# Transposing attention output by the DMA crossbar in a fused sliding/dilated attention and MLP kernel

## The chip, the cores and the metric

The kernel runs on one core of a Trainium2 chip. The metric is device time in microseconds, the median of repeated executions; less is better. The profile is of one execution on the same core.

## The reference

Attention over 8 batch rows, 8 heads, 576 positions, head dimension 64, followed by an MLP with a squared ReLU over all 4608 tokens. Heads 0 to 3 look back over a window of 32 positions; heads 4 to 7 look back over 128 positions and see every fourth one.

```python
batch, n_heads, seq, head_dim = (8, 8, 576, 64)
rel = pos[:, None] - pos[None, :]
mask_plain = (rel >= 0) & (rel < 32)
mask_dil = (rel >= 0) & (rel < 128) & (rel % 4 == 0)
attn = softmax(where(mask, q @ k.T / 8, -1e9));  o = attn @ v
x = o.transpose(0, 2, 1, 3).reshape(4608, 512)
g = np.maximum(x @ w_in, 0) ** 2        # w_in: 512 x 2048
out = g @ w_out                          # w_out: 2048 x 512
```

Inputs and output are float32; the kernel computes with float16 operands and float32 sums.

## The kernel before

**Two streams of work on TensorE.** The attention of one batch row (index `b`, 0 to 7) is interleaved by hand with the MLP of one chunk of 512 tokens. The MLP of chunk `c` is a Python generator (`moe_gen`) that issues a few matmuls and then yields; `pump(n)` lets it run n steps. From chunk 2 on a chunk has 60 steps: 32 for the first matrix product (`mm1_gen`: two for each of 16 blocks of the hidden dimension) and 28 for the second (`mm2_strassen_gen`, which uses seven half-size products in the PSUM banks `pa`, `pb` and `pc`). Bank `pa` is filled four times: after each filling ScalarE copies it out (`take`, line 387, tiles `ou` and `ov`), and the next filling must wait for that copy. The fillings end with steps 36, 42, 50 and 56.

While row `b` is computed, the pending generator is that of chunk `b - 1`. Tokens are numbered row after row, 576 to a row, so chunk `b - 1` needs rows up to `b - 1` alone, and chunk `b` needs the first `512 - 64 b` tokens of row `b`.

**One row of attention**, in program order:

- `pump(first)`: 24, 16, then 8 steps for rows 2, 3 and 4 on.
- `attn_scores`: `s_sliding` twice, `s_dilated` twice; each makes scores transposed (keys on partitions), then ScalarE's exponential (line 547) and VectorE's product with a mask (line 548). Each is followed by `pump(gap)`, with gap 4 in row 2 and 3 later.
- `attn_values`: three `av_sliding` (each two blocks of 96 queries, four heads) and four `av_dilated` (queries of two of the four residue classes, halves `t` of 72 queries). `normalize` divides by the softmax sum on VectorE (lines 590 and 591) and gives x with tokens on partitions. `x_sliding` (tile `px`) and `x_dilated` (tile `py`) transpose x on TensorE into PSUM, and ScalarE copies it to `xT` (lines 640 and 658). `xT` has features on partitions, as the first MLP product wants it, and keeps four rows of tokens. `pump(gap2)` stands between the parts, with 2 in row 2 and 3 later.
- `pump(1000)`: the rest of the chunk's steps.

**Loads.** For row `b + 1`, during row `b`: GpSimd's queue loads q and k of the sliding heads (`ns`) and rewrites those of the dilated ones in DRAM (`dd`), after `after_transposes` has seen the last QK transpose of the row before land (`seen`, line 231). At hook 3, after the second `s_dilated`, `turn` runs: `by_token` on VectorE reorders `ns` to `nr`; then SyncE's queue issues the write of `nr` to DRAM (`dp`), the loads of v (`sv`, `sd`), the DMA transposes of `dp` into `QKTp` and of `dd` into `QKTd`; GpSimd casts v (`cast_v`). The results of each chunk (`leave`, tiles `ou`, `ov`) are stored by SyncE's queue too.

Rows 0 and 1 are written out separately: they transpose q and k on TensorE and run before or between the first chunks.

PSUM: two tiles of two banks for attention (`pa` by function name, tag "pa"), and four single banks for the MLP and for `px` and `py` (tag "pm").

Of the kernel before, what the change touches and what calls it, by code (L numbers as in the profile page):

```python
# [17 lines left out]
def kernel(  # L18
# [28 lines left out]
    NB = S // QB  # L47
    PADP = P - QB
    CL = S // DIL
    QD = CL // 2  # L50
    PADD = (48, P - QD)
    OWND = (CL - 64, 64)
    KPAD = 64
    UW = 576

# [1 line left out]
    wpool = ctx.enter_context(tc.tile_pool(name="wpool", bufs=1))  # L57
    stg = ctx.enter_context(tc.tile_pool(name="stg", bufs=1))
    natp = ctx.enter_context(tc.tile_pool(name="natp", bufs=2))
    xp = ctx.enter_context(tc.tile_pool(name="xp", bufs=4))  # L60
    gp = ctx.enter_context(tc.tile_pool(name="gp", bufs=2))
    osb = ctx.enter_context(tc.tile_pool(name="osb", bufs=3))
    otp = ctx.enter_context(tc.tile_pool(name="otp", bufs=3))
# [68 lines left out]

    def load_dilated_v(b, eng):
        vv = v[b, HH:H].rearrange("h (i c) d -> i h (c d)", c=DIL)
        i0 = 0
        for t in range(2):
            eng.dma_start(out=sd[P - OWND[t] : P, t, :, :], in_=vv[i0 : i0 + OWND[t]])
            i0 += OWND[t]

    def load_v(b):  # L140
        load_sliding_v(b)
# [114 lines left out]
    md = maskd.rearrange("p (n t w) -> p n t w", t=2, w=QD)  # L256
    for m, w, pad in (
        (maskp.rearrange("p (n w) -> p n w", w=QB), QB, PADP),
        (md[:, :, 0], QD, PADD[0]),
        (md[:, :, 1], QD, PADD[1]),  # L260
    ):
# [305 lines left out]
    def s_dilated(b, g):  # L567
        tiles = [pa(f"pz{b}_{g}_{h}") for h in range(2)]
        for h, ps in enumerate(tiles):
            for a in range(2):  # L570
                for t in range(2):
                    q0 = KPAD + (2 * g + h) * CL + QD * t
                    for e in range(2):
                        r = slice(D * e, D * (e + 1))
                        n = 2 * a + t
                        nc.tensor.matmul(  # L576
                            ps[:, e, QD * n : QD * (n + 1)],
                            QKTd[b % 2][r, 1, a, q0 - PADD[t] : q0 - PADD[t] + P],
                            QKTd[b % 2][r, 0, a, q0 : q0 + QD],
                            start=True,  # L580
                            stop=True,
                        )
        for h, ps in enumerate(tiles):
            softmax(4 + 2 * g + h, ps, maskd)

    def normalize(b, what, pav, w):
        x = xp.tile([QB, 2, HH, D], FP16, name=f"x{b}_{what}", tag="x")
        rcp = xp.tile([QB, 2, HH], FP32, name=f"rcp{b}_{what}", tag="rcp")
        pv = pav[0:w, :, 0 : HH * (D + 2)].rearrange("p i (h d) -> p i h d", d=D + 2)
        nc.vector.reciprocal(rcp[0:w], pv[:, :, :, D])  # L590
        nc.vector.tensor_tensor(  # L591
            out=x[0:w],
            in0=pv[:, :, :, 0:D],
            in1=rcp[0:w].unsqueeze(3).to_broadcast([w, 2, HH, D]),
            op=ALU.mult,
        )
        return x

    def av_sliding(b, mp):
# [12 lines left out]
        return normalize(b, f"p{mp}", pav, QB)  # L612

    def av_dilated(b, t, a):
        pav = pa(f"paw{b}_{t}_{a}")
        for e in range(2):
            for h in range(HH):
                off = e * 288 + a * 144 + t * QD
# [7 lines left out]
        return normalize(b, f"d{t}_{a}", pav, QD)  # L626

    def x_sliding(b, half, xs, wide):
        px = pt(f"px{b}_{half}", wide)
        for m3 in range(3):  # L630
            m = 3 * half + m3
            x = xs[m // 2][:, m % 2].rearrange("p h d -> p (h d)")
            for c in range(2):
                nc.tensor.transpose(  # L634
                    px[:, 288 * c + QB * m3 : 288 * c + QB * (m3 + 1)],
                    x[:, P * c : P * (c + 1)],
                    ident[0:QB, 0:QB],
                )
        t0 = (b * S + 288 * half) % XW
        nc.scalar.copy(  # L640
            xT[:, 0:2, t0 : t0 + 288],
            px[:, 0:UW].rearrange("x (c t) -> x c t", c=2),
        )

    def x_dilated(b, t, xs, wide):
        py = pt(f"py{b}_{t}", wide)
        for a in range(2):
            for e in range(2):
                x = xs[a][:, e].rearrange("p h d -> p (h d)")
                for c in range(2):  # L650
                    o = 288 * c + QD * (2 * a + e)
                    nc.tensor.transpose(  # L652
                        py[:, o : o + QD],
                        x[0:QD, P * c : P * (c + 1)],
                        ident[0:QD, 0:QD],
                    )
        t0 = (b * S + 288 * t) % XW
        nc.scalar.copy(  # L658
            xT[:, 2:4, t0 : t0 + 288].rearrange("x c (i r) -> x c i r", r=DIL),
            py[:, 0:UW].rearrange("x (c r i) -> x c i r", c=2, r=DIL),  # L660
        )

    def attn_scores(b, gap, less=0, hooks={}):
        for hp in range(2):
# [10 lines left out]
            pump(gap - less)  # L675

    def attn_values(b, gap, wide=False, hooks={}):
        xs = []
        for mp in range(3):
            xs.append(av_sliding(b, mp))  # L680
            if mp < 2:
                halo_sliding(b, mp + 1)
            else:
                halo_dilated(b, 0)
            if 4 + mp in hooks:
                hooks[4 + mp]()
            pump(gap)
        x_sliding(b, 0, xs, wide)
        halo_dilated(b, 2)
        pump(gap)  # L690
        ys = [av_dilated(b, 0, 0)]
        pump(gap)
        x_sliding(b, 1, xs, wide)
        pump(gap)
        ys.append(av_dilated(b, 0, 1))
        pump(gap)
        zs = []
        for a in range(2):
            zs.append(av_dilated(b, 1, a))
            pump(gap)  # L700
        x_dilated(b, 0, ys, wide)
        pump(gap)
        x_dilated(b, 1, zs, wide)


    n, m = nsd[0]
# [16 lines left out]
        t_dilated(0, m, a, False)  # L723
    halo_sliding(0, 1)
    pump(1)
    xs = [av_sliding(0, 0)]
    pump(1)
    for g in range(2):
        s_dilated(0, g)
# [14 lines left out]
    dd = keep_dilated_qk(2)  # L744
    nr = by_token(2, ns)
    for mp in (1, 2):
        xs.append(av_sliding(0, mp))
        pump(1)
    x_sliding(0, 0, xs, False)
    pump(1)  # L750
    ys = [av_dilated(0, 0, 0)]
    pump(1)
    x_sliding(0, 1, xs, False)
    pump(1)
    pending.clear()
# [30 lines left out]
    for b in range(2, B):  # L786
# [56 lines left out]
```

The softmax here doesn't subtract the row's maximum and nothing guards it: scores larger than these inputs give would overflow.

## Time and profile before

| | |
|---|---|
| median of 3 runs | 311.45 us (311.31 to 311.76) |
| profiled execution | 309.11 us, its span on the core 307.3 us |
| TensorE busy | 290.7 us (95%) |
| VectorE, ScalarE, GpSimd busy | 207.9, 183.4, 71.7 us |
| px transposes (line 634) | 96, with ScalarE copies of 0.638 us to `xT`, 16 |
| py transposes (line 652) | 128, with ScalarE copies of 0.638 us to `xT`, 16 |
| QKTp, QKTd DMA transposes | 12 each, 288 KB, median to landing 6.5 and 3.9 us |
| TensorE clock granted | full throughout |

The span reaches from the first to the last instruction; the time also has what lies around it. In the profile a group is named by line, engine and operation, then what it writes and reads (`xT<-py`), with buffer numbers left out. SPq is SyncE issuing DMAs; a time to landing runs from the start of the issue until all data has arrived. Consecutive matmuls overlap, so the time that a group costs TensorE is the distance from its start to the start of the next one, not the duration of one.

### The profile page before, as it was taken

To read this page: it belongs to the slowest core of one execution; us is meant where nothing else is said; L and a number is where in the kernel's file an instruction comes from. 1 tells how busy PE (TensorE), PEld (TensorE's weight loads), DVE (VectorE), ACT (ScalarE), POOL (GpSimd) and SP (SyncE) were. 2 spreads that over 40 slices of the span, in tenths; PEclk is the share of its full clock that TensorE was granted. 3 is DMA by queue.
4 is the path that set the end of the run, shared out by engine and by line. 5 is a ranking of instruction groups with operands and counts; after the bars stand their busy time and mean duration, and the time that the engine had idled before them with its cause. 6 is when DMAs were issued, how large, how long until landed. Compare 5 with 4: busy or idle time off the path is not lost.

```text
span 307.3 us, 7108 instructions
## 1 busy us (share of the span) xinstructions
PE 290.7 (95%) x2874; PEld 196.5 (64%) x2874; DVE 207.9 (68%) x433; ACT 183.4 (60%) x326; POOL 71.7 (23%) x114
## 2 busy tenths in 40 slices
PE   1798998999999999999999999999999999999994
PEld 1454554554455469656998997569756975785583
DVE  7784448568953798489748983898378934834652
ACT  2766648668645982598339834983499336425620
POOL 4481008413805303400630083007000000000000
PEclk9999999999999999999999999999999999999999
DMA  7899997999699999999968996889500020003004
GB/s 116 188 200 213 206 171 114 189 241 205 112 214 194 222 199 185 240 154 191 171 130 188 181 184 97 219 166 186 165 10 2 0 109 29 0 4 136 2 0 137
DMA packets 67024, 43.58 MB, mean 142 GB/s; under 512 B 48624, under 2 KB 59376, under 8 KB 66992
## 3 DMA queue, kind: packets, MB, share of 16 engines
q1 hardware_dynamic: 57920, 28.45, 44.9%
q0 software_dynamic: 9072, 14.68, 27.7%
q8 instruction: 22, 0.36, 0.5%
q14 instruction: 10, 0.08, 0.1%
HBM read 36.70 MB, written 16.52 MB: 173 GB/s over the span
## 4 chain that ended last, share of the span: by engine, by line
PE 71%; ACT 10%; DVE 7%; DMA 6%; issue 2%; SPq 2%; POOL 1%; POOLq 0%; DVEq 0%
PE ph L294 27%; PE pa L371 16%; PE pb L371 8%; PE po L437 7%; ACT AT L547 5%; DMA ns<-in_q_dram 5%; PE pc L371 4%; ACT rt L317 3%; PE paw L619 3%; PE pav L605 2%; PE px L634 1%; PE py L652 1%; DVE AT L548 1%; DMA QKTp<-dp 1%; PE pf L491 1%
## 5 line engine op out<-in xcount | busy, mean ns | idle before, releaser
L294 PE MATMUL ph<-xT,wi 128*128 128x512 f16 (+1 forms) x640 | 133.4, 359 | 0.7 <-ACT xT L658 0.7
L317 ACT ACTIVATE rt<-ph 128x512 f16<-128x512 f32 x144 | 84.9, 603 | 33.5 <-PE ph L294 33.5
L294 PEld LDWEIGHTS <-wi 128*128 128x128 f16 x640 | 68.6, 114 | 46.8 <-issue 0.8
L318 DVE TENSOR_TENSOR g<-rt 128x512 f16<-128x512 f16 x144 | 62.2, 435 | 42.7 <-ACT rt L317 41.1
L371 PEld LDWEIGHTS <-g 128*128 128x128 f16 x448 | 42.5, 98 | 5.3
L170 POOL CAST vp<-sv 128x512 f16<-128x512 f32 x24 | 17.5, 760 | 108.6 <-DMA sv<-in_v_dram 62.1
L371 PEld LDWEIGHTS <-gs 128*128 128x128 f16 x336 | 31.6, 98 | 3.7 <-DVE gs L328 0.3
L437 PE MATMUL po<-wo,g 128*128 128x512 f16 x128 | 33.1, 379 | 0.0
L398 DVE TENSOR_TENSOR ov<-pb,ov 128x512 f32<-128x512 f32 x14 | 9.7, 691 | 29.9 <-PE pb L371 18.2
L371 PE MATMUL pa<-wt,gs 128*128 128x256 f16 x224 | 28.5, 273 | 0.0
L371 PE MATMUL pb<-wt,g 128*128 128x256 f16 x224 | 27.7, 273 | 0.0
L178 POOL CAST vd<-sd 128x512 f16<-128x512 f32 (+1 forms) x32 | 24.2, 782 | 3.1 <-DMA sd<-in_v_dram 2.4
L387 ACT COPY ov<-pa 128x512 f32<-128x512 f32 x14 | 8.2, 585 | 26.8 <-PE pa L371 26.8
L591 DVE TENSOR_TENSOR x_d<-paw,rcp_d 72x512 f16<-72x512 f32 x32 | 22.0, 687 | 1.1
L547 ACT ACTIVATE AT<-pz 128x576 f16<-128x576 f32 x32 | 20.0, 712 | 1.7 <-PE pz L576 1.6
L548 DVE TENSOR_TENSOR AT<-AT,maskp 128x576 f16<-128x576 f16 x32 | 17.3, 545 | 5.1 <-ACT AT L547 2.6
L547 ACT ACTIVATE AT<-ps 128x576 f16<-128x576 f32 x32 | 19.2, 662 | 1.2 <-PE ps L557 0.9
L658 ACT COPY xT<-py 128x576 f16<-128x576 f16 x16 | 10.2, 640 | 14.7 <-PE py L652 14.6
L591 DVE TENSOR_TENSOR x_p<-pav,rcp_p 96x512 f16<-96x512 f32 x24 | 16.5, 687 | 0.8
L387 ACT COPY ou<-pa 128x512 f32<-128x512 f32 x14 | 8.2, 588 | 14.5 <-PE pa L371 14.5
L548 DVE TENSOR_TENSOR AT<-AT,maskd 128x576 f16<-128x576 f16 x32 | 14.9, 484 | 2.6 <-ACT AT L547 0.6
L640 ACT COPY xT<-px 128x576 f16<-128x576 f16 x16 | 10.2, 638 | 9.2 <-PE px L634 8.6
(81 smaller groups left out, 306.6 us busy)
## 6 DMA issues: line engine op xcount, KB each, us to landing
sv<-in_v_dram SPq DMA_DIRECT2D x14, 288.0 KB, 6.2
dp<-nr SPq DMA_DIRECT2D x12, 288.0 KB, 4.1
out_dram<-ou SPq DMA_DIRECT2D x6, 512.0 KB, 3.1
out_dram<-ov SPq DMA_DIRECT2D x6, 512.0 KB, 3.5
sd<-in_v_dram SPq DMA_DIRECT2D x8, 320.0 KB, 7.3
ns<-in_k_dram POOLq DMA_DIRECT2D x8, 288.0 KB, 5.2
ns<-in_q_dram POOLq DMA_DIRECT2D x8, 288.0 KB, 6.4
sd<-in_v_dram SPq DMA_DIRECT2D x8, 256.0 KB, 6.7
```

Of the source, the lines that this page charges most:

```text
L170: nc.gpsimd.tensor_copy(vp[b % 2][:, m : m + 2, :, 0:D], sv[:, :, m : m + 2, :].rearrange("p h m d -> p m h d"))
L178: nc.gpsimd.tensor_copy(vd[b % 2][p0:P, t, c : c + 2, :, 0:D], sd[p0:P, t, :, D * c : D * (c + 2)].rearrange("p h (c d) -> p c h d", d=D),)
L294: nc.tensor.matmul(ph[:, t0:t1], wi4[ffc // 4][:, dmk, :, ffc % 4], xT[:, dmk, x0 : x0 + t1 - t0], start=(dmk == 0 and t0 == 0), stop=(dmk ...
L317: nc.scalar.activation(rt, ph[:], ACTF.Relu)
L318: nc.vector.tensor_mul(g[:, ffc, :], rt, rt)
L371: nc.tensor.matmul(banks[bank][:, t], a(k, t), b(k), start=(new and t == 0 and k == 0), stop=(k == HF - 1), skip_group_check=True,)
L387: nc.scalar.copy(ot, banks[A])
L437: nc.tensor.matmul(po, g[:, ffc, t * P : (t + 1) * P], wo[ffc // 4][:, ffc % 4, :], start=(ffc == 0), stop=(ffc == NFF - 1),)
L547: nc.scalar.activation(AT[:, u, 0:UW], ps[:, :, 0 : UW // 2], ACTF.Exp, scale=scale)
L548: nc.vector.tensor_mul(AT[:, u, 0:UW], AT[:, u, 0:UW], mask)
L591: nc.vector.tensor_tensor(out=x[0:w], in0=pv[:, :, :, 0:D], in1=rcp[0:w].unsqueeze(3).to_broadcast([w, 2, HH, D]), op=ALU.mult,)
L640: nc.scalar.copy(xT[:, 0:2, t0 : t0 + 288], px[:, 0:UW].rearrange("x (c t) -> x c t", c=2),)
```

## The change

From row 3 on, `attn_values_by_dma` takes the place of `attn_values`. x stays in SBUF tiles with tokens on partitions, and four DMA transposes a row (SBUF to SBUF, issued by SyncE) take the place of 28 PE transposes. The two of the sliding heads write straight into `xT`. The two of the dilated heads write a tile `yd` in which each residue class is contiguous; ScalarE then interleaves the classes into `xT` (`x_from`). Rows 0 to 2 keep the PE transposes.

The halves of a residue class's 144 queries become 80 and 64, in place of 72 and 72 (`QD`, `Q0D`, `PADD`), in all rows; masks, scores, values and transposes follow. `normalize` writes into tiles that `x_tiles` gives: `xs` (96 x 2 x 6 x 2 x 64) and `xd` (80 or 64 x 4 x 4 x 64), two buffers of each.

`turn` is cut in three. At hook 3 it still reorders, writes `dp` and loads v. `turned` (the QKTp transposes) comes after the sliding x transposes, and `done` (the QKTd transposes and the casts of v) after the dilated ones. In row 2 both follow `attn_scores` at once.

```diff
-    QD = CL // 2
-    PADD = (48, P - QD)
-    OWND = (CL - 64, 64)
+    QD = (80, 64)
+    Q0D = (0, 80)
+    PADD = (48, 64)
...
-    xp = ctx.enter_context(tc.tile_pool(name="xp", bufs=4))
+    xp = ctx.enter_context(tc.tile_pool(name="xp", bufs=2))
+    yp = ctx.enter_context(tc.tile_pool(name="yp", bufs=1))
...
-                    q0 = KPAD + (2 * g + h) * CL + QD * t
+                    q0 = KPAD + (2 * g + h) * CL + Q0D[t]
...
-                            ps[:, e, QD * n : QD * (n + 1)],
+                            ps[:, e, o : o + QD[t]],
...
-    def normalize(b, what, pav, w):
-        x = xp.tile([QB, 2, HH, D], FP16, name=f"x{b}_{what}", tag="x")
...
+    def normalize(b, what, pav, w, x):
...
+        if x.shape[2] < HH:
+            pv, rb = [y.rearrange("p i (c e) d -> p i c e d", c=2) for y in (pv, rb)]
+        nc.vector.tensor_tensor(out=x, in0=pv, in1=rb, op=ALU.mult)
...
+    def x_tiles(b):
+        x = xp.tile([QB, 2, NB, 2, D], FP16, name=f"xs{b}", tag="xs")
+        return x, [xp.tile([QD[t], DIL, HH, D], FP16, name=f"xd{b}_{t}", tag=f"xd{t}") for t in range(2)]
...
+    def x_from(b, t, y):
+        t0 = b * S % XW + DIL * Q0D[t]
+        o = xT[:, 2:4, t0 : t0 + DIL * QD[t]].rearrange("x c (i r) -> x c i r", r=DIL)
+        nc.scalar.copy(o, y.rearrange("x r c i -> x c i r"))
+
+    def x_sliding_by_dma(b, xs):
+        t0 = b * S % XW
+        for c in range(2):
+            nc.sync.dma_start_transpose(
+                out=xT[:, c, t0 : t0 + S].rearrange("x (m q) -> x m q", q=QB),
+                in_=xs[0][:, c].rearrange("p m e d -> p (m e d)"),
+            )
+
+    def x_dilated_by_dma(b, t, xs):
+        y = yp.tile([P, DIL, 2, QD[t]], FP16, name=f"yd{b}_{t}", tag=f"yd{t}")
+        nc.sync.dma_start_transpose(
+            out=y.rearrange("x r c i -> x (r c) i"), in_=xs[1][t].rearrange("p r h d -> p (r h d)")
+        )
+        return y
...
+    def attn_values_by_dma(b, gap, then=(None, None)):
+        xs = x_tiles(b)
+        for mp in range(3):
+            av_sliding(b, mp, xs)
+            if mp < 2:
+                halo_sliding(b, mp + 1)
+            else:
+                for c in (0, 2):
+                    halo_dilated(b, c)
+            pump(gap)
+        x_sliding_by_dma(b, xs)
+        if then[0]:
+            then[0]()
+        ys = []
+        for t in range(2):
+            for a in range(2):
+                av_dilated(b, t, a, xs)
+                pump(gap)
+            ys.append(x_dilated_by_dma(b, t, xs))
+        if then[1]:
+            then[1]()
+        for t in range(2):
+            pump(7 if b > 3 else 5)
+            x_from(b, t, ys[t])
...
             def turn():
-                dp = keep_sliding_qk(nxt, by_token(nxt, ns))
+                kept.append(keep_sliding_qk(nxt, by_token(nxt, ns)))
                 load_v(nxt)
-                transpose_sliding(nxt, dp)
+
+            def turned():
+                transpose_sliding(nxt, kept[0])
+
+            def done():
                 transpose_dilated(nxt, dd)
                 cast_v(nxt)
...
-        attn_values(b, gap2, False, hooks)
+        if b == 2:
+            turned()
+            done()
+            attn_values(b, gap2)
+        else:
+            attn_values_by_dma(b, gap2, (turned, done) if nxt < B else (None, None))
```

More of the change, by code (lines that the diff above doesn't have):

```diff
@@ L134, in load_dilated_v @@
         vv = v[b, HH:H].rearrange("h (i c) d -> i h (c d)", c=DIL)
-        i0 = 0
         for t in range(2):
-            eng.dma_start(out=sd[P - OWND[t] : P, t, :, :], in_=vv[i0 : i0 + OWND[t]])
-            i0 += OWND[t]
+            eng.dma_start(out=sd[P - QD[t] : P, t, :, :], in_=vv[Q0D[t] : Q0D[t] + QD[t]])
     def load_v(b):
@@ L255 @@
     hi_ = const.tile([P, QB], FP16, name="hi_")
-    md = maskd.rearrange("p (n t w) -> p n t w", t=2, w=QD)
+    md = maskd.rearrange("p (n w) -> p n w", w=CL)
     for m, w, pad in (
         (maskp.rearrange("p (n w) -> p n w", w=QB), QB, PADP),
-        (md[:, :, 0], QD, PADD[0]),
-        (md[:, :, 1], QD, PADD[1]),
+        (md[:, :, 0 : QD[0]], QD[0], PADD[0]),
+        (md[:, :, QD[0] : CL], QD[1], PADD[1]),
     ):
@@ L571, in s_dilated @@
                 for t in range(2):
-                    q0 = KPAD + (2 * g + h) * CL + QD * t
+                    q0 = KPAD + (2 * g + h) * CL + Q0D[t]
                     for e in range(2):
                         r = slice(D * e, D * (e + 1))
-                        n = 2 * a + t
+                        o = CL * a + Q0D[t]
                         nc.tensor.matmul(
-                            ps[:, e, QD * n : QD * (n + 1)],
+                            ps[:, e, o : o + QD[t]],
                             QKTd[b % 2][r, 1, a, q0 - PADD[t] : q0 - PADD[t] + P],
-                            QKTd[b % 2][r, 0, a, q0 : q0 + QD],
+                            QKTd[b % 2][r, 0, a, q0 : q0 + QD[t]],
                             start=True,
@@ L584, in s_dilated, with av_sliding @@
             softmax(4 + 2 * g + h, ps, maskd)
-    def normalize(b, what, pav, w):
-        x = xp.tile([QB, 2, HH, D], FP16, name=f"x{b}_{what}", tag="x")
-        rcp = xp.tile([QB, 2, HH], FP32, name=f"rcp{b}_{what}", tag="rcp")
+    def normalize(b, what, pav, w, x):
+        rcp = xp.tile([P, 2, HH], FP32, name=f"rcp{b}_{what}", tag="rcp")
         pv = pav[0:w, :, 0 : HH * (D + 2)].rearrange("p i (h d) -> p i h d", d=D + 2)
         nc.vector.reciprocal(rcp[0:w], pv[:, :, :, D])
[L591 to L599, printed above, removed]
+        pv = pv[:, :, :, 0:D]
+        rb = rcp[0:w].unsqueeze(3).to_broadcast([w, 2, HH, D])
+        if x.shape[2] < HH:
[4 more added lines that the diff above has]
+        return x, [xp.tile([QD[t], DIL, HH, D], FP16, name=f"xd{b}_{t}", tag=f"xd{t}") for t in range(2)]
+    def av_sliding(b, mp, xs):
         pav = pa(f"pav{b}_{mp}")
@@ L611, in av_sliding, with av_dilated @@
                 )
-        return normalize(b, f"p{mp}", pav, QB)
-    def av_dilated(b, t, a):
+        normalize(
+            b, f"p{mp}", pav, QB, xs[0][:, :, 2 * mp : 2 * mp + 2].rearrange("p c m e d -> p m c e d")
+        )
+    def av_dilated(b, t, a, xs):
         pav = pa(f"paw{b}_{t}_{a}")
@@ L617, in av_dilated @@
             for h in range(HH):
-                off = e * 288 + a * 144 + t * QD
+                off = e * 288 + a * CL + Q0D[t]
                 nc.tensor.matmul(
@@ L625, in av_dilated @@
                 )
-        return normalize(b, f"d{t}_{a}", pav, QD)
+        normalize(b, f"d{t}_{a}", pav, QD[t], xs[1][t][:, 2 * a : 2 * a + 2])
     def x_sliding(b, half, xs, wide):
@@ L630, in x_sliding @@
         for m3 in range(3):
-            m = 3 * half + m3
-            x = xs[m // 2][:, m % 2].rearrange("p h d -> p (h d)")
             for c in range(2):
@@ L635, in x_sliding @@
                     px[:, 288 * c + QB * m3 : 288 * c + QB * (m3 + 1)],
-                    x[:, P * c : P * (c + 1)],
+                    xs[0][:, c, 3 * half + m3].rearrange("p e d -> p (e d)"),
                     ident[0:QB, 0:QB],
@@ L646, in x_dilated @@
         py = pt(f"py{b}_{t}", wide)
[L647 to L660, printed above, removed]
+        w = QD[t]
+        for r in range(DIL):
+            x = xs[1][t][:, r].rearrange("p h d -> p (h d)")
+            for c in range(2):
+                o = w * (2 * r + c)
+                nc.tensor.transpose(py[:, o : o + w], x[:, P * c : P * (c + 1)], ident[0:w, 0:w])
+        x_from(b, t, py[:, 0 : 8 * w].rearrange("x (r c i) -> x r c i", r=DIL, c=2))
+    def x_from(b, t, y):
[4 more added lines that the diff above has]
+        t0 = b * S % XW
+        for c in range(2):
+            nc.sync.dma_start_transpose(
[6 more added lines that the diff above has]
+            out=y.rearrange("x r c i -> x (r c) i"), in_=xs[1][t].rearrange("p r h d -> p (r h d)")
         )
+        return y
     def attn_scores(b, gap, less=0, hooks={}):
@@ L677, in attn_values @@
     def attn_values(b, gap, wide=False, hooks={}):
-        xs = []
+        xs = x_tiles(b)
         for mp in range(3):
-            xs.append(av_sliding(b, mp))
+            av_sliding(b, mp, xs)
             if mp < 2:
@@ L684, in attn_values @@
                 halo_dilated(b, 0)
-            if 4 + mp in hooks:
-                hooks[4 + mp]()
             pump(gap)
@@ L690, in attn_values @@
         pump(gap)
-        ys = [av_dilated(b, 0, 0)]
+        av_dilated(b, 0, 0, xs)
         pump(gap)
@@ L694, in attn_values @@
         pump(gap)
-        ys.append(av_dilated(b, 0, 1))
+        av_dilated(b, 0, 1, xs)
         pump(gap)
-        zs = []
         for a in range(2):
-            zs.append(av_dilated(b, 1, a))
+            av_dilated(b, 1, a, xs)
             pump(gap)
-        x_dilated(b, 0, ys, wide)
+        x_dilated(b, 0, xs, wide)
         pump(gap)
-        x_dilated(b, 1, zs, wide)
+        x_dilated(b, 1, xs, wide)
+    def attn_values_by_dma(b, gap, then=(None, None)):
+        xs = x_tiles(b)
+        for mp in range(3):
+            av_sliding(b, mp, xs)
+            if mp < 2:
[18 more added lines that the diff above has]
+            x_from(b, t, ys[t])
     n, m = nsd[0]
@@ L725 @@
     pump(1)
-    xs = [av_sliding(0, 0)]
+    xs = x_tiles(0)
+    av_sliding(0, 0, xs)
     pump(1)
@@ L746 @@
     for mp in (1, 2):
-        xs.append(av_sliding(0, mp))
+        av_sliding(0, mp, xs)
         pump(1)
@@ L750 @@
     pump(1)
-    ys = [av_dilated(0, 0, 0)]
+    av_dilated(0, 0, 0, xs)
     pump(1)
@@ L755 @@
     pending.clear()
-    ys.append(av_dilated(0, 0, 1))
-    zs = [av_dilated(0, 1, 0)]
+    av_dilated(0, 0, 1, xs)
+    av_dilated(0, 1, 0, xs)
     begun = [mm1_begin(0, 0)]
-    zs.append(av_dilated(0, 1, 1))
+    av_dilated(0, 1, 1, xs)
     begun.append(mm1_begin(0, 1))
-    x_dilated(0, 0, ys, False)
-    x_dilated(0, 1, zs, False)
+    x_dilated(0, 0, xs, False)
+    x_dilated(0, 1, xs, False)
     g0 = hidden(0)
@@ L797, in turn @@
             def turn():
-                dp = keep_sliding_qk(nxt, by_token(nxt, ns))
+                kept.append(keep_sliding_qk(nxt, by_token(nxt, ns)))
                 load_v(nxt)
-                transpose_sliding(nxt, dp)
+            def turned():
+                transpose_sliding(nxt, kept[0])
+            def done():
                 transpose_dilated(nxt, dd)
                 cast_v(nxt)
+            kept = []
             hooks[3] = turn
```

## The prediction

> **What bounds the kernel now.** I read the page's busy lines first, then the windows of one row in the steady part (row 5, 157.3 to 188.5 us), then the timelines of TensorE, ScalarE and the DMA queue there.
>
> The page: TensorE is the engine to relieve.
>
> ```profile
> PE 290.7 (95%) x2874; PEld 196.5 (64%) x2874; DVE 207.9 (68%) x433; ACT 183.4 (60%) x326; POOL 71.7 (23%) x114
> ```
>
> Windows inside row 5 (columns: length; busy of PE, PEld, DVE, ACT, POOL; clock; mean packets in flight per DMA engine; GB/s). TensorE has no holes, so its own microseconds count. The DMA engines are idle until 170, then full for 15 us, and idle again at 186.
>
> ```profile
> 168.00:169.00 1.00, 0.90 (x15) 0.80 (x13) 1.00 (x3) 1.00 (x3) 0.00 (x0) 1.00 0.00 0
> ...
> 170.00:180.00 10.00, 10.00 (x129) 9.51 (x127) 9.60 (x20) 6.30 (x12) 2.30 (x2) 1.00 1.13 191
> 180.00:185.00 5.00, 5.00 (x66) 4.54 (x64) 3.34 (x7) 2.06 (x4) 4.31 (x6) 1.00 1.08 208
> ...
> 186.00:187.00 1.00, 1.00 (x12) 0.90 (x10) 0.07 (x1) 0.00 (x0) 0.62 (x2) 1.00 0.02 8
> ```
>
> What fills them is SyncE's queue, in this order (timeline: start, length of the issue), and the time to landing of the last kinds:
>
> ```profile
> 169.10 1.14 SPq L212 DMA_DIRECT2D dp<-nr  x2
> 170.33 2.31 SPq L131 DMA_DIRECT2D sv<-in_v_dram  x2
> 172.73 1.97 SPq L137 DMA_DIRECT2D sd<-in_v_dram  x2
> 174.81 5.77 SPq L220 DMA_TRANSPOSE QKTp<-dp  x2
> 180.67 2.99 SPq L224 DMA_TRANSPOSE QKTd<-dd  x2
> ```
>
> ```profile
> sd<-in_v_dram SPq DMA_DIRECT2D x1, 256.0 KB, 6.8
> QKTp<-dp SPq DMA_TRANSPOSE x2, 6.8
> QKTd<-dd SPq DMA_TRANSPOSE x2, 3.8
> ```
>
> The last sd was issued at 174.0 and so landed at 180.8; the second QKTp, issued at 176.4, took 6.7 and landed at 183.05; the last QKTd at 185.8. They land one after another.
>
> TensorE and ScalarE at the end of row 5 (timelines). py is a group of eight PE transposes. The bank pa is filled, ScalarE copies it to ov, and only then may the pa product of 185.10 begin: it began 0.36 us after that copy's end at 184.74.
>
> ```profile
> 182.39 0.42 PE L652 MATMUL py<-ident,x_d 72*128 72x72 f16 x8
> 182.65 1.48 PE L371 MATMUL pa<-wt,gs 128*128 128x256 f16 x12
> 183.96 0.42 PE L652 MATMUL py<-ident,x_d 72*128 72x72 f16 x8
> 184.22 1.04 PE L371 MATMUL pc<-wo,g 128*128 128x256 f16 x8
> 185.10 1.91 PE L371 MATMUL pa<-wo,gs 128*128 128x256 f16 x16
> ```
>
> ```profile
> 182.85 0.64 ACT L658 COPY xT<-py 128x576 f16<-128x576 f16 x1 [2.11 <-PE py L652]
> 184.16 0.58 ACT L387 COPY ov<-pa 128x512 f32<-128x512 f32 x1 [0.67 <-PE pa L371]
> 184.64 0.65 ACT L658 COPY xT<-py 128x576 f16<-128x576 f16 x1
> ```
>
> **What the Trainium skill says.** "VectorE: DVE Perf Modes", The three transpose paths, prices a 128x128 transpose at 390 ns on TensorE and 1309 ns on the crossbar. As a cost of TensorE this trace disagrees: a lone py shows 197 ns, but the next product starts 0.26 us after eight of them begin (182.39 to 182.65). "Advanced Engine Details and Errata", X-Bar Transpose (TRN2), expects crossbar transposes at 350 to 400 GB/s; the window 181 to 185, with nothing else in flight, shows 222 GB/s, and I use that. "DMA: Bandwidth & Descriptors", Queues, rings and completion order, says that an engine takes its ring's descriptors in order; the successive landings above agree. So a new transfer on SyncE's queue waits out what was issued before it.
>
> **The change, part by part**, in row 5's clock.
>
> *Removed from TensorE, rows 3 to 7.* Four groups of transposes a row: px at 172.99, followed by the next matmul at 173.25, a second px, and two py. Each takes 0.26 us of issue, together 1.04 us; five rows give **-5.2 us**. TensorE is full there, so all of it counts if nothing new makes it wait.
>
> *Removed from ScalarE.* Two px copies of 0.638 us a row. The two py copies become copies of 640 and 512 elements from SBUF. By slope, between the SBUF copies of line 185 (256 elements 0.402, 512 elements 0.602), they take 0.70 and 0.60 us, the same sum. 1.28 us a row less on ScalarE; counted as nothing, since TensorE is full anyway.
>
> *VectorE.* The products of line 591 keep count and 512 elements (0.687 us); only the write pattern differs. Zero, bounded by +-0.1 us each, hidden in a VectorE that is 68% busy. The 80/64 split keeps the number of matmuls and their columns (2 x 72 = 80 + 64), and the sum of rows 0 to 2's copies. Zero: +-0.3 us overall.
>
> *Added to SyncE's queue, rows 3 to 7.* Two sliding transposes of 96 x 768 elements and two dilated of 80 x 1024 and 64 x 1024. The present transposes move 256-byte packets (window 181 to 185: 3564 packets, 0.89 MB), 1152 for 288 KB. The four of row 5 landed between 180.8 and 185.8, so 4608 packets took 5.0 us, 1.08 ns each. The new ones have 576 + 576, 640 and 512 packets: 1.25, 0.70 and 0.55 us. Issue on SyncE: the present ones take 1.3 us unhindered and up to 4.2[...], so the issue hides behind the transfers. SyncE also waits for VectorE now: for the last sliding product (done 174.73, when the loads' issue has just ended at 174.70) and for the dilated ones. Behind those waits stand QKTp, QKTd and the stores of `out` (187.66 and 189.51 now); a store late by 1 us costs nothing, as its tile is written again a chunk later. No SBUF-to-SBUF transpose is in this trace. Bounds: 18 ns a packet on 16 engines, the best quarter microsecond (294 GB/s, 0.87 ns), or twice 1.08. I take 1.08, as the packets are the same.
>
> *The order on that queue.* dp, sv, sd, sliding x, QKTp, dilated x 0, dilated x 1, QKTd. Dilated x 0 is ready before it matters: VectorE finishes x_d of t=0 at 180.3 now, about 179.2 then. It must wait out sd (180.8), sliding x 1.25, QKTp (183.05 - 180.8 = 2.25) and itself 0.70: **landed at 185.0**.
>
> *The new wait.* The ScalarE copy of it (`x_from`, t=0) stands after 8+12+9+12+7 = 48 of the 60 steps of the MLP generator; the third pa product is steps 47 to 50, its copy to ov comes in step 50, the fourth pa product begins with step 53. ScalarE works in order, so that copy to ov is queued behind `x_from`, and TensorE's fourth pa product behind that. Landing 185.0, plus start 0.12 (as QKTd landing at 185.77 and its reader at 185.89), 0.70 copy, 0.04, 0.585 copy to ov, 0.06: TensorE may go on at 186.5. Without a wait it would be there at 185.10 - 1.04 = 184.06. **Stall 2.45 us, row 5.** The second `x_from`, seven steps later, finds its data (185.0 + 0.55) landed.
>
> *The other rows, alike.* Row 4: QKTp landed at 152.35, x 154.3, on at 155.8, due at 153.82 - 1.04: 3.0. Row 6: 214.6, 216.5, 218.0, due 216.28 - 1.04: 2.8. Row 3 has `x_from` six steps later, at step 54, but its DMA runs later still (QKTp landed at 125.45, x at 127.4). There the second half of the next chunk's first matmul needs `x_from` (done 128.2), due at 126.13 - 1.04 + 0.43 = 125.5; then 0.2 more until the bank behind is copied: 2.9. Row 7 has no loads or QKT transposes: x ready at 241.6, landing after about 3.0 (the least for the double size is 3.5), wanted by 246.5 - 1.5: no stall.
>
> *Moved.* QKTp and QKTd of the next row land about 1.25 and 2.5 us later. QKTd gates `seen` and so the next ns loads on GpSimd's queue: they start 0.6 us later against the next row, whose own start moves 1.4, but ns lands (163.5) 4.8 us before VectorE's `by_token` reads it (168.32). Cover enough. Row 2's store passing ahead of QKTp: nothing waits for it.
>
> Sum: -5.2 + 2.9 + 3.0 + 2.45 + 2.8 = **+6.0 us**. The profiled execution took 309.11 us (span 307.3 and 1.8 around it), so it would take 315.1; the median shown is 311.45, so **317.4 us**. With stalls each 1 us less or more: 313.4 to 321.4.
>
> **Rivals.** *In time (faster).* If dilated x 0 lands by 182.6 in row 5 (184.06 - 1.46), no stall remains and -5.2 us stand: 306.3. For it: TensorE is full, and each row has some 6 us in which the DMA engines are idle (167.7 to 170, 185.2 to 188). Against it: sd alone lands at 180.8, and even at 0.87 ns a packet the sum is 184.2. It decides where the transfers ahead shrink by 2.4 us. Smaller gains, up to 310.8, belong here.
>
> *Crossbar from SBUF at half the rate.* 1.95 us more ahead of `x_from` in each of four rows: 7.8 more, 325.2. For it: reads and writes meet on SBUF. Against it: packets of the same size.
>
> *Break-even.* Stalls of about 1.3 us in four rows (4 x 1.3 = 5.2): 311.4; needs landings 1.5 us earlier.
>
> *That it doesn't do what it says:* if these transposes were run as element-wise copies, DMA time would grow many times; part of the slow rival.
>
> **How the numbers follow.** Late landing and stalled TensorE 0.60, half rate or worse 0.11, in time 0.24, break-even 0.05. So slower by over 0.2% (about what a measurement can tell here) 0.71, same 0.05, faster 0.24. The likeliest case's own range is 313.4 to 321.4. To hold 8 in 10 the range goes down to 307.5, which leaves out about half of the in-time case, and up to 323, which leaves out most of the half-rate case: together 2 in 10.
>
> **What would show it.** In the profile after: no px or py from row 3 on; in rows 4 to 6 a wait of ScalarE on the yd transposes of 2 us or more before `x_from`, then TensorE idle about 2.5 us before a pa product of line 371, and in row 3 before ph; dilated x 0 landing about 2 us after the second QKTp; rows 4 to 6 longer by 1.4 to 2 us each; row 7 about 1 us shorter. I am wrong if TensorE stays full in rows 3 to 6, or if x lands ahead of QKTp.

## The result and the profile after

| | before | after |
|---|---|---|
| median of 4 runs | 311.38 us (309.20 to 311.76) | **322.02 us** (319.78 to 322.92) |
| ratio | 1 | 1.0353, 95% interval 1.0290 to 1.0416 |
| profiled execution | 309.11 us, span 307.3 | 319.78 us, span 318.0 |

The change costs 10.6 us by the medians and 10.7 by the profiled executions; 6.0 had been forecast. The page's first line of the kernel after, as before (busy us, share of the span, instructions): TensorE is busy 1.0 us less in a span that is 10.7 us longer, so it waits.

```profile
PE 289.7 (91%) x2734; PEld 192.1 (60%) x2734; DVE 206.0 (65%) x433; ACT 183.4 (58%) x316; POOL 74.7 (23%) x114
```

What it waits for, from the waits of the kernel after (engine, line, tile, what it waited for; total us, times, longest). Together 13.2 us; before, the third stood at 0.7, the fourth at 0.4 and the first two were not there. The waits for the first loads are left out here.

```profile
PE pa L370 <- ACT ov L386: 5.5, 3, 1.9
PE paw L621 <- DVE xd L593: 3.4, 4, 0.8
PE ph L293 <- ACT xT L658: 2.4, 3, 1.1
PE paw L621 <- DVE rcp_d L588: 1.9, 2, 1.5
```

Behind the first stands a wait of ScalarE, from ScalarE's waits of the kernel after:

```profile
ACT xT L658 <- DMA yd<-xd: 14.8, 4, 3.9
```

The chain in row 5, which now begins at 163.35 (157.31 before). First SyncE's queue (start, length of the issue): x has come in ahead of QKTp and ahead of QKTd.

```profile
178.96 1.96 SPq L137 DMA_DIRECT2D sd<-in_v_dram  x2
181.02 2.55 SPq L663 DMA_TRANSPOSE xT<-xs  x2
183.67 3.80 SPq L219 DMA_TRANSPOSE QKTp<-dp  x2
187.56 3.32 SPq L670 DMA_TRANSPOSE yd<-xd  x2
190.99 3.04 SPq L223 DMA_TRANSPOSE QKTd<-dd  x2
```

By their times to landing, the last sd landed at 186.08, the second sliding x at 187.14, the two QKTp at 189.5 and 190.4, and dilated x 0 at 191.42. ScalarE's timeline shows what stands still meanwhile: nothing for 3.63 us, then `x_from`, and only behind it the copy of the third `pa` product. TensorE's timeline: that product is finished at 190.69, yet the fourth begins at 193.24. (A bracket is the idle time before the group and what ended it.)

```profile
191.44 1.26 ACT L658 COPY xT<-yd 128x640 f16<-128x640 f16 x1 [3.63 <-DMA yd<-xd]
192.61 0.58 ACT L386 COPY ov<-pa 128x512 f32<-128x512 f32 x1
```

```profile
183.16 1.04 PE L370 MATMUL pc<-wo,g 128*128 128x256 f16 x8
185.03 0.41 PE L621 MATMUL paw<-vd,AT 128*128 128x65 f16 x8 [0.83 <-DVE xd L593]
...
188.78 1.91 PE L370 MATMUL pa<-wt,gs 128*128 128x256 f16 x16
190.52 1.04 PE L370 MATMUL pc<-wo,g 128*128 128x256 f16 x8
193.24 1.91 PE L370 MATMUL pa<-wo,gs 128*128 128x256 f16 x16 [1.68 <-ACT ov L386]
```

The windows give the same in numbers (length; busy of PE, PEld, DVE, ACT, POOL; clock; packets in flight per DMA engine; GB/s): in the 5.4 us up to the landing ScalarE works 0.59 us, and in the 1.8 us after it TensorE works 0.16. The DMA engines have a mean of 1.08 packets each in flight up to the landing: the queue is at work for most of the time, and x is late in it. (A mean hides what happens inside: for about 1 us of this stretch next to nothing moved, as the section on the prediction shows.)

```profile
186.00:191.40 5.40, 5.40 (x51) 4.84 (x50) 2.74 (x6) 0.59 (x1) 4.46 (x6) 1.00 1.08 177
191.40:193.20 1.80, 0.16 (x2) 0.00 (x0) 0.00 (x0) 1.76 (x3) 0.00 (x0) 1.00 0.68 108
```

A row's length below is the distance between the first `ph` products of two chunks.

| us | start of row 3 | row 3 | row 4 | row 5 | row 6 | row 7 |
|---|---|---|---|---|---|---|
| before | 94.38 | 31.75 | 31.18 | 31.28 | 31.18 | 31.20 |
| after | 95.39 | 32.31 | 35.65 | 33.38 | 33.54 | 31.50 |
| difference | +1.0 | +0.6 | +4.5 | +2.1 | +2.4 | +0.3 |

Row 3's own stall falls just behind the `ph` that begins row 4 and so counts there.

### The profile page after: what moved, and what is told of

It reads as the page before. It is cut to its first block, busy times and chain, and to the rows that moved or that the text cites. A ratio compares the mean times of both kernels' runs of the same rounds, so it can differ in the third digit from the quotient of the medians.

```text
span 318.0 us, 6874 instructions
## 1 busy us (share of the span) xinstructions
PE 289.7 (91%) x2734; PEld 192.1 (60%) x2734; DVE 206.0 (65%) x433; ACT 183.4 (58%) x316; POOL 74.7 (23%) x114
## 3 DMA queue, kind: packets, MB, share of 16 engines
q1 hardware_dynamic: 70080, 31.40, 49.0%
## 4 chain that ended last, share of the span: by engine, by line
PE 48%; DVE 20%; ACT 12%; DMA 11%; issue 5%; SPq 2%; POOL 1%; DVEq 0%; POOLq 0%
PE ph L293 19%; PE pa L370 9%; PE po L436 6%; DMA ns<-in_q_dram 6%; PE pb L370 5%; ACT AT L546 5%; DMA yd<-xd 4%; DVE g L317 3%; DVE xs L593 3%; ACT rt L316 3%; DVE xd L593 3%; ACT xT L658 2%; DVE gs L326 2%; DVE gs L327 2%; DVE g L401 1%
## 5 line engine op out<-in xcount | busy, mean ns | idle before, releaser
L317 DVE TENSOR_TENSOR g<-rt 128x512 f16<-128x512 f16 x144 | 60.9, 428 | 45.0 <-ACT rt L316 44.0
L169 POOL CAST vp<-sv 128x512 f16<-128x512 f32 x24 | 20.8, 897 | 100.2 <-DMA sv<-in_v_dram 85.6
L370 PEld LDWEIGHTS <-gs 128*128 128x128 f16 x336 | 32.4, 98 | 9.9 <-issue 6.0
L370 PE MATMUL pa<-wt,gs 128*128 128x256 f16 x224 | 27.1, 273 | 0.0
L370 PE MATMUL pb<-wt,g 128*128 128x256 f16 x224 | 26.9, 273 | 0.0
L593 DVE TENSOR_TENSOR xd<-paw,rcp_d 80x512 f16<-80x512 f32 (+1 forms) x32 | 21.9, 684 | 1.1
L658 ACT COPY xT<-yd 128x640 f16<-128x640 f16 (+1 forms) x10 | 11.8, 1181 | 14.9 <-DMA yd<-xd 14.8
L621 PEld LDWEIGHTS <-AT 128*128 128x128 f16 x256 | 11.4, 97 | 13.2 <-issue 6.1
L621 PE MATMUL paw<-vd,AT 128*128 128x65 f16 x256 | 13.2, 193 | 6.0 <-DVE xd L593 3.4
L370 PE MATMUL pa<-wo,gs 128*128 128x256 f16 x112 | 13.4, 272 | 5.5 <-ACT ov L386 5.5
```

The source lines that it names most:

```text
L169: nc.gpsimd.tensor_copy(vp[b % 2][:, m : m + 2, :, 0:D], sv[:, :, m : m + 2, :].rearrange("p h m d -> p m h d"))
L317: nc.vector.tensor_mul(g[:, ffc, :], rt, rt)
L370: nc.tensor.matmul(banks[bank][:, t], a(k, t), b(k), start=(new and t == 0 and k == 0), stop=(k == HF - 1), skip_group_check=True,)
L593: nc.vector.tensor_tensor(out=x, in0=pv, in1=rb, op=ALU.mult)
L621: nc.tensor.matmul(pav[:, e, h * (D + 2) : h * (D + 2) + D + 1], AT[:, 4 + h, off : off + P], vd[b % 2][:, t, 2 * a + e, h, 0 : D + 1], st ...
L658: nc.scalar.copy(o, y.rearrange("x r c i -> x c i r"))
```

## The experiments

Each was timed against the kernel before on the same chip, whose median there was 310.4 to 310.6 us. "After" as a base for a difference is 322.02; it stood beside a kernel before of 311.38, so such a difference holds to about 1 us. A ratio is to the kernel before.

**1. The layout alone.** Classes of 80 and 64, new x tiles, but x transposed on TensorE in all rows, and the QKT transposes at hook 3 again.

```diff
             def turn():
                 kept.append(keep_sliding_qk(nxt, by_token(nxt, ns)))
                 load_v(nxt)
+                turned()
+                done()
...
-        if b == 2:
-            turned()
-            done()
-            attn_values(b, gap2)
-        else:
-            attn_values_by_dma(b, gap2, (turned, done) if nxt < B else (None, None))
+        attn_values(b, gap2)
```

> The changed kernel with PE transposes in every row and the old place of the QKT transposes: only the 80/64 split, the new x tiles and the pool sizes are left of the change. Late-landing theory and short-spacing theory: the time of the kernel before, 311.4 us, within 0.7, with rows of 31.2 us and no TensorE wait of over 0.3 us in rows 3 to 7. Layout theory (the new split or write pattern costs something, for instance the 1 us by which row 2 began later after the change): 312.4 us or more, up to 316.

Measured: 311.53 us, ratio 1.0034 (1.0015 to 1.0052), rows 4 to 7 of 31.4 to 31.5. Costed at nothing, the layout costs this kernel 1.0 us. In row 5 TensorE takes the same steps as before, but for the two groups of `py` (timeline of this kernel; the lines of before are in the prediction):

```profile
183.85 0.45 PE L652 MATMUL py<-ident,xd 80*128 80x80 f16 x8
184.14 1.48 PE L370 MATMUL pa<-wt,gs 128*128 128x256 f16 x12
185.55 0.40 PE L652 MATMUL py<-ident,xd 64*128 64x64 f16 x8
185.88 1.05 PE L370 MATMUL pc<-wo,g 128*128 128x256 f16 x8
```

From the first `py` to the `pc` product takes 2.03 us, in place of 1.83. The same 0.2 us in each of rows 3 to 7 makes up the 1.0. The changed kernel has no `py` from row 3 on, so its 10.6 us does not contain this cost, except for what rows 0 to 2 have of it.

**2. The matmuls between the parts put back.** With the two `px` gone, the two `pump(gap)` behind them were gone too, and the four `av_dilated` follow each other more closely. Here both pumps come back, and `x_from` keeps its place in the chunk (in row 3 the first comes one step later).

```diff
         ys = []
+        pump(gap)
         for t in range(2):
             for a in range(2):
                 av_dilated(b, t, a, xs)
                 pump(gap)
+                if t == 0 and a == 0:
+                    pump(gap)
...
-            pump(7 if b > 3 else 5)
+            pump(((1, 7) if b > 3 else (0, 4))[t])
```

> The changed kernel with MLP steps put back between the dilated value blocks, where px stood; x_from stays at step 48 and 55. Late-landing theory: in rows 4 to 6 the row ends when the transposed x has landed, so TensorE only waits longer before the fourth pa product, by about what it saves before paw; 0 to -2.5 us in all, from rows 3 and 7 alone: 319.5 to 322. Short-spacing theory (a value block waits for VectorE to empty one of two PSUM tiles, 0.84 to 1.45 us a row, and that is the loss): -5 us, about 317.

Measured: 325.56 us, ratio 1.0474 (1.0418 to 1.0530), 3.5 slower than after. No theory had this. The waits of `paw` on VectorE are gone, and row 7, which has no stall of its own, is 0.85 shorter (30.65). In rows 4 to 6 it gains nothing: later `av_dilated` means later x, and the waits before `pa` grow. TensorE's timeline of this kernel shows a further price: the same 16 products take about 3.17 us in place of 1.91 after two of the three gaps.

```profile
162.02 3.17 PE L370 MATMUL pa<-wo,gs 128*128 128x256 f16 x16 [3.16 <-ACT ov L386]
197.39 3.18 PE L370 MATMUL pa<-wo,gs 128*128 128x256 f16 x16 [3.31 <-ACT ov L386]
232.51 1.91 PE L370 MATMUL pa<-wo,gs 128*128 128x256 f16 x16 [3.54 <-ACT ov L386]
```

So the `paw` waits were hidden in rows 4 to 6 behind a landing that was later still: taking away the earlier of two waits lengthens the later one.

The further price is TensorE's clock, granted at half for a while after a gap (last section). The four runs here have a mean granted clock of 0.974 to 0.984, those of after 0.989 to 1.000. The missing share times the span is 5.2 to 8.5 us, an upper estimate of what it cost. That is more than the 3.5: at full clock this kernel would by this estimate take 319 to 320 us, close to the 319.5 to 322 of the late-landing theory.

**3. Dilated x 0 ahead of QKTp.**

```diff
-        if then[0]:
-            then[0]()
...
             ys.append(x_dilated_by_dma(b, t, xs))
+            if t == 0 and then[0]:
+                then[0]()
```

> The changed kernel with the QKTp transposes issued after the first dilated x transpose and not ahead of it. Late-landing theory: yd of t=0 lands 2 to 3 us earlier, the waits before the fourth pa product (1.7 to 1.9 us, three rows) and most of that before ph in row 3 (1.75) go: -6 to -8 us, 314 to 316, with the waits before paw left. Short-spacing theory: 0 to -1 us, 321 to 322. Rival that the crossbar is slow from SBUF whatever stands ahead of it: less than -3 us.

Measured: 314.13 us, ratio 1.0101 (1.0044 to 1.0159): about 8 us better than after by one change of order. In row 5 dilated x 0 lands 26.1 us into the row (186.1, the row starting at 160.07) in place of 28.1, and all three waits before `pa` are gone; rows 4 to 7 are 33.40 (with row 3's stall), 31.55, 31.50 and 31.51. The `paw` waits are left, and so is row 3's wait before `ph` (1.59), most of which should have gone. That shows the order on the queue as the main cause.

**4. Both edits together** (2 and 3).

> Both edits of e2 and e3. Late-landing theory: the gain of e3, and now the waits before paw count as well, since nothing later holds the row: -9 to -13 us, 309 to 313, more than the two gains added. If the two are independent: the sum of e2 and e3. Short-spacing theory: as e2, about 317.

Measured: 317.70 us, ratio 1.0214 (1.0129 to 1.0299), 3.6 worse than 3 alone, where better was expected. With the pumps back, dilated x 0 of row 5 lands 27.1 us into the row (192.73, the row starting at 165.63), 1.0 later than in 3, while `x_from` stays at step 48: the waits before `pa` return, with 2.02, 2.01 and 0.93 us in rows 4 to 6. Two of these gaps were again followed by half clock (TensorE's timeline of this kernel):

```profile
160.47 3.03 PE L370 MATMUL pa<-wo,gs 128*128 128x256 f16 x16 [2.02 <-ACT ov L386]
194.55 2.96 PE L370 MATMUL pa<-wo,gs 128*128 128x256 f16 x16 [2.01 <-ACT ov L386]
```

Most of the 3.6 goes with this clock. Two of the four runs took 315.32 and 315.77 us with a mean clock of 1.000 and 0.995, the other two 319.63 and 319.85 with 0.989 and 0.984; hence the wide interval. The run without any loss of clock is 1.2 above the median of 3. The lesson of 2 and 4: the pumps make x later, and are worth having only if the reader moves later too.

**5. What TensorE would gain at best.** Experiment 1, without x from row 4 on.

```diff
     def x_sliding(b, half, xs, wide):
+        if b > 3:
+            return
...
     def x_dilated(b, t, xs, wide):
+        if b > 3:
+            return
```

> e1 with the transposes of x and their copies to xT left out from row 4 on (xT keeps older tokens there). It prices what the change takes from TensorE. Step of the prediction: four groups of 0.26 us in each of four rows, -4.2 us against e1 (311.5): 307 to 307.5, rows of 30.3 us. Rival (the groups are hidden by other waits, or pay more than their issue): within 1 us of e1, or below 306.

Measured: 307.24 us, 4.3 less than experiment 1; rows 4 to 7 are 30.14 to 30.23, where experiment 1 had 31.40 to 31.48 and the kernel before 31.18 to 31.28. So a row without the transposes is 1.25 us shorter than in experiment 1, whose `py` are dearer, and 1.04 to 1.05 shorter than before. Against the kernel before that is what the prediction counted (1.04), and five rows could save 5.2.

**6. The copy in the other order of elements,** to read SBUF in sequence and write with a stride.

```diff
-        nc.scalar.copy(o, y.rearrange("x r c i -> x c i r"))
+        nc.scalar.copy(o.rearrange("x c i r -> x r c i"), y)
```

> The changed kernel with x_from's copy walking yd in its stored order and writing xT with a stride of four elements, in place of reading with a stride and writing in order. x_from took 1.27 and 1.09 us where 0.70 and 0.60 were forecast. If the strided read from SBUF is what costs: 0.7 and 0.6 us, and since the copy stands in the chain that ends rows 3 to 6, -2 to -2.5 us against the changed kernel: 319 to 320. If it is the source in SBUF or the four-dimensional pattern: both near 1.1 to 1.3 us still, 321 to 323.

Measured: 326.39 us, ratio 1.0510 (1.0467 to 1.0554): slower still, which neither case had. The copies by tile, of after (from `py` in PSUM, rows 0 to 2, and from `yd` in SBUF) and of this kernel (ns: least, median, most):

```profile
L658 ACT COPY xT<-py x6: 586/639/697, 24.7 to 93.8; 128x640 f16<-128x640 f16 x3, 128x512 f16<-128x512 f16 x3
L658 ACT COPY xT<-yd x10: 1056/1180/1305, 127.7 to 258.1; 128x640 f16<-128x640 f16 x5, 128x512 f16<-128x512 f16 x5
```

```profile
L658 ACT COPY xT<-py x6: 1383/1498/1588, 23.7 to 96.1; 128x640 f16<-128x640 f16 x3, 128x512 f16<-128x512 f16 x3
L658 ACT COPY xT<-yd x10: 1312/1476/1623, 130.6 to 262.6; 128x640 f16<-128x640 f16 x5, 128x512 f16<-128x512 f16 x5
```

With the stride on the reading side, 640 elements take 0.69 us from PSUM and 1.27 from SBUF; with the stride on the writing side, 1.58 from PSUM and 1.61 from SBUF. The forecast took its price from copies within SBUF without a stride (512 elements of 32 partitions 0.602, about the 0.59 from PSUM). So neither the source in SBUF nor the stride by itself costs here, but a stride on a side that lies in SBUF, and more where it is written.

As a time the run says less: the edit also slowed the six copies from `py` in rows 0 to 2, and the mean granted clock was 0.978 to 0.995, up to 1.6 to 7.2 us of the span by the estimate of experiment 2.

**7. `x_from` later:** both at step 56, in row 3 too.

```diff
-            pump(7 if b > 3 else 5)
+            pump(((15, 0) if b > 3 else (7, 0))[t])
```

> The changed kernel with both x_from copies after the copy that frees bank pa for the last time (step 56), order of the queue unchanged. ScalarE-order theory: yd still lands as late, but no copy of a pa bank is queued behind it: the waits before the fourth pa product in rows 4 to 6 go (1.92, 1.68, 1.88), row 3's before ph stays: -5 to -6 us, 316 to 317. If TensorE waited for the crossbar in another way: within 1.5 us of the changed kernel, 320.5 to 323.5.

Measured: 315.56 us, ratio 1.0165 (1.0144 to 1.0186), 6.5 better than after, with every transfer where it was. The waits before `pa` are gone (TensorE's timeline of this kernel, row 5); the late copy now costs 0.56 in this row, at the next `ph`.

```profile
188.20 1.04 PE L370 MATMUL pc<-wo,g 128*128 128x256 f16 x8
189.08 1.91 PE L370 MATMUL pa<-wo,gs 128*128 128x256 f16 x16
...
193.94 2.32 PE L293 MATMUL ph<-xT,wi 128*128 128x512 f16 x10 [0.56 <-ACT xT L658]
```

3 and 7 cut the same chain at different links, the landing and its reader in ScalarE's order, and each alone takes all three waits before `pa` away. That chain is therefore shown.

**8. All of x ahead of both QKT transposes, with the pumps and a later `x_from`.**

```diff
-        if then[0]:
-            then[0]()
         ys = []
+        pump(gap)
...
+                if t == 0 and a == 0:
+                    pump(gap)
             ys.append(x_dilated_by_dma(b, t, xs))
+        if then[0]:
+            then[0]()
         if then[1]:
             then[1]()
         for t in range(2):
-            pump(7 if b > 3 else 5)
+            pump(((9, 2) if b > 3 else (1, 2))[t])
```

> All four crossbar transposes of x ahead of QKTp and QKTd, the MLP steps between the value blocks as before the change, x_from after step 56. Late-landing theory: nothing waits any more except some of row 3: rows 4 to 7 of 30.2 to 30.6 us, 306 to 309, faster than before. Rival (the DMA queue is now the bound: QKTd lands 3 to 4 us into the next row, ns loads begin after it, by_token and dp come late and each row is held by the loads): rows of 31.5 us or more, 312 or more.

Measured: 312.39 us, ratio 1.0064 (1.0037 to 1.0090), where 306 to 309 had been expected; what was named as the rival came about. Rows 6 and 7 reach 30.9, but row 3's late transfers come back in row 4: QKTd lands 7.8 us into row 4, `seen` lets GpSimd load `ns` only then, and VectorE's `by_token` is late. From VectorE's timeline of this kernel, and TensorE's a little later:

```profile
141.35 0.76 DVE L120 COPY nr<-ns 128x2304 f16<-128x2304 f16 x1 [2.75 <-DMA ns<-in_q_dram]
```

```profile
143.76 0.42 PE L605 MATMUL pav<-vp,AT 128*128 128x65 f16 x8 [2.00 <-ACT rt L316]
```

The cover of 4.8 us that the prediction named for these loads is limited. In after it was down to 0.8 us in row 4 (`ns` landed at 139.90 and was read at 140.73), and here it is used up: what is moved behind x in one row has to be paid by the next row's loads.

**9. The same from row 4 on; row 3 keeps TensorE,** with its QKT transposes at hook 3, and `x_from` at steps 51 and 56.

```diff
-            pump(7 if b > 3 else 5)
+            pump((4, 5)[t])
...
                 load_v(nxt)
+                if b < 4:
+                    turned()
+                    done()
...
-        if b == 2:
-            turned()
-            done()
+        if b < 4:
             attn_values(b, gap2)
```

> A version that the runs so far point to: row 3 keeps its PE transposes (its loads end latest against its end), rows 4 to 7 use the crossbar with all four x transposes ahead of the QKT ones, MLP steps between the value blocks, x_from at steps 51 and 56. Late-landing theory: from e1's 311.5 each of four rows loses the 1.25 us that e5 measured: 306.5 to 308 us, 1 to 1.3% faster than before, rows 4 to 7 of 30.2 to 30.5 us. Rival (the row's loads are the bound once TensorE's row is shorter): rows 5 and 6 of 31 us or more, 309 to 312.

Measured: **307.20 us (6 runs, 305.90 to 307.81), ratio 0.9890 (0.9859 to 0.9922)**, faster than the kernel before by 1.1%, and by some 14.5 us than after. Rows 30.14, 30.23, 30.87 and 30.14: as short as without any transposes, but for row 6, which loses 0.7 us in small delays between its value blocks (the profile shows one, a wait of 0.2 us on VectorE). In its ScalarE timeline `x_from` follows the copy of `pa` and waits for nothing:

```profile
184.21 0.58 ACT L386 COPY ov<-pa 128x512 f32<-128x512 f32 x1 [3.16 <-PE pa L370]
184.81 1.30 ACT L658 COPY xT<-yd 128x640 f16<-128x640 f16 x1
```

## Why the prediction was right, and where its sizes were off

**The mechanism was right.** ScalarE in rows 4 to 6 waits on `yd` (3.6 to 3.9 us), the copy of `pa` is queued behind, TensorE idles before the fourth `pa` product and in row 3 before `ph`; rows 5 and 6 grew by 2.1 and 2.4 us. TensorE's saving of 1.04 us a row was right as well (experiment 5 against the kernel before). The step from the profiled execution to the median, 2.3 us, was 2.2. The sum was too small: 322.02 lies above the likeliest case's own range, 313.4 to 321.4. It is inside the whole range thanks to the part up to 323, which was added for a crossbar at half the rate, and that did not happen: that much is luck. The terms that were too small follow; by row the forecast was +1.9, +2.0, +1.4, +1.8 and -1.0 for rows 3 to 7.

**Row 5 (forecast +1.4, measured +2.1).** Its end is set by the landing and the copies behind it, so the miss can be read as two terms, from the row's start. The landing was forecast at 185.0 - 157.31 = 27.7 and came at 191.42 - 163.35 = 28.1: +0.4. Within that, sd landed 0.8 earlier in the row, and the step from sd to dilated x took 5.3 us and not 4.2. The two sliding x took 1.1 (1.25 forecast), and here "Advanced Engine Details and Errata", X-Bar Transpose (TRN2), which expects 350 to 400 GB/s, is again above the trace: 0.53 us between the two landings of 147 KB is 278 GB/s. But QKTp, of the same size as before, needed 3.3 us in place of 2.25. The windows inside it (of after, columns as above) show why: a hole of about 1 us, in which TensorE goes on and the DMA engines move next to nothing.

```profile
188.25:189.25 1.00, 1.00 (x12) 0.90 (x10) 0.56 (x1) 0.00 (x0) 1.00 (x1) 1.00 0.32 21
189.25:190.41 1.16, 1.16 (x13) 1.04 (x11) 0.00 (x0) 0.00 (x0) 1.10 (x3) 1.00 1.16 237
```

Just ahead of it, at 187.5, starts a packet of 16 KB on the queue that the DMA view calls `instruction`. Rows 4 and 6 of after have the same hole in QKTp, and row 3 has it between the two sliding x (landed at 122.86 and 124.86), each time behind such a packet. The kernel before has it too, in rows 3 and 6: there QKTp also needed 3.3 us from sd's landing (122.19 to 125.47, 211.31 to 214.59). Row 5 of before, from which 2.25 was read, had none in its transposes. So the 1.0 us is not a cost of the new transposes. That the packet causes the hole is read from the times alone, and not tested.

From landing to TensorE's going on took 1.8 us, 1.5 forecast: **`x_from` was mis-sized**, 1.26 us and not 0.70, because its price came from contiguous copies. It started 0.1 sooner after the landing than allowed for, and ScalarE's next copy overlaps its end, so 0.3 of it shows. 0.4 + 0.3 is the miss of 0.7. The stall of 2.45 itself shows in two parts, 0.83 before `paw` and 1.68 before `pa`. Row 6 missed by as much, +2.4 against 1.8, but its forecast already held a hole (QKTp 3.3 us in both kernels); there sd landed 0.6 later in the row. And the prediction's sign that dilated x 0 lands about 2 us after the second QKTp did not fit its own sum, which has 0.70 between them; measured were 0.7 to 1.0.

**Row 3 and row 4 (forecast +3.8, measured +5.0).** The prediction said that the second `x_from` finds its data landed, and counted nothing for it. In row 3 it does cost, as the timeline at the start of row 4 shows (TensorE, then ScalarE, kernel after):

```profile
128.98 0.38 PE L293 MATMUL ph<-xT,wi 128*128 128x512 f16 x1 [0.69 <-ACT xT L658]
130.42 1.89 PE L293 MATMUL ph<-xT,wi 128*128 128x512 f16 x8 [1.06 <-ACT xT L658]
```

```profile
127.65 1.28 ACT L658 COPY xT<-yd 128x640 f16<-128x640 f16 x1 [3.53 <-DMA yd<-xd]
...
129.31 1.06 ACT L658 COPY xT<-yd 128x512 f16<-128x512 f16 x1
```

The next matmul waits for the second copy to end at 130.37, though chunk 3 reads columns 1536 to 2047 of `xT` and that copy writes 2048 to 2303. It writes two feature blocks of one tile, and the other columns of the second block lie between its first and last element; that the dependence covers the whole stretch is an argument, not tested. With its two waits before `ph` (1.75) counted to it, row 3 grew by 2.3 us, and row 4 by 2.7; the latter missed as row 5 did, by a hole in QKTp and a longer `x_from`.

**Row 7 (forecast -1.04, measured +0.3).** No stall on x, as forecast: `yd` landed 2.7 us after its issue, about 3.0 forecast (from a least time of QKTd that is 3.60, not 3.5). But a wait was missed: `paw` waits for VectorE (0.8 us at a time, line 593). `av_dilated` uses two tiles in turn, and with `px` and its pump gone they come faster than `normalize` empties them. Where nothing later hides it, it eats the saving; experiment 2 gets 0.85 of it back in row 7.

**Layout (0 forecast): 0.2 us a row where x is transposed on TensorE** (experiment 1), so none from row 3 on. **Start of row 3 (0 forecast): +1.0.** Row 2's first `ph` came anywhere from 61.0 to 64.0 us in the profiled executions of experiments 1 to 4 and 6, so the 1.0 is not shown to belong to the change.

**The rivals.** Half rate from SBUF did not happen (0.53 us for 576 packets). "In time" did not happen as written, but what would have made it true was near: one reordering (3) or one later copy (7) removes the stalls, and experiment 9 ends on that side.

## What to carry to other kernels

Work moved to a queue in order is late by all that stands ahead of it, and whoever waits for it holds up all that is queued behind the waiter, on an engine that has nothing to do with the transfer: so order the transfers by when their readers need them, and put the reader behind the copies that free other engines' buffers. Moves of the producer and of the reader belong together (2 and 4 against 9). Removing matmuls also removes cover: what the removed group was hiding becomes the next wait. And before a difference of a few microseconds is given a cause, look at the granted clock of each run (2, 4 and 6).

## What was not expected of the hardware

**Short gaps can halve TensorE's clock.** After waits of 2.02 and 2.01 us (4) and of 3.16 and 3.31 us (2), 16 products took 2.96 to 3.18 us in place of 1.91, at a granted clock of half. It is not a matter of length alone: after 1.92 us (row 4 of after) and after 3.54 us (row 6 of 2) they took 1.91. "TensorE: Matmul & The Clock Gate", Why this matters for your kernels, advises against idle gaps above about 3 us; here 2.0 was enough in 4, and 3.54 did no harm in 2.

The traces show more. Every half-clock stretch between the start and the end of a profiled execution lasts 3.41 us, and the full-clock stretches between two of them are whole multiples of that (8 and 9 times in 2, 9 times in 4). So in these runs the clock changes on a grid of 3.41 us, and what can be counted is how long TensorE was busy in each step of it. Windows of 2 on that grid, two pairs of neighbours:

```profile
159.06:162.47 3.41, 0.45 (x5) 0.40 (x5) 0.47 (x1) 2.25 (x3) 0.12 (x1) 1.00 0.76 145
162.47:165.88 3.41, 3.41 (x19) 2.35 (x17) 0.82 (x2) 1.07 (x2) 0.44 (x2) 0.50 0.53 88
...
227.33:230.74 3.41, 1.63 (x15) 1.31 (x14) 0.24 (x1) 0.03 (x1) 1.89 (x3) 1.00 1.06 219
230.74:234.15 3.41, 1.64 (x16) 1.47 (x16) 1.29 (x2) 2.71 (x3) 0.00 (x0) 1.00 0.82 141
```

In the first pair TensorE is busy for 0.45 of 3.41 us, and the next step is at half clock. The gap of 3.54 us lies across both steps of the second pair, each is busy for 1.6, and full clock stays. The other steps ahead of half clock were busy for 0.89 and 1.11 us (2), 1.39 and 1.40 (4) and 1.49 (6, at its start); the 1.92 us gap of after lies in a step with 1.49, and full clock stayed. So the limit lies near 1.4 to 1.5 us of 3.41 by this count, which takes modelled ends of matmuls. So where a gap falls on the grid counts too, and not its length alone.

**Strided copies and short transposes.** ScalarE's copy of 640 two-byte elements with an interleave takes 0.69 us when it reads PSUM, 1.27 when it reads SBUF, and 1.6 when the stride is on the SBUF side written to. And a crossbar transpose from SBUF to SBUF with nothing ahead of it still needs 2.5 to 2.7 us from issue to landing (row 7 of after: first sliding x 2.53, dilated x 2.68 and 2.65).
